# A three-stage kernel (attention, dense layer, top-2 mixture of experts): the list table in bfloat16 parts, the last batch's routing spread, the first expert's low halves on GpSimd

## The chip, the cores and the metric

The kernel runs on one core of a Trainium2 chip. The metric is device time in microseconds (us), the median over runs of one program. TensorE (PE in the profile, with its weight loads as PEld), VectorE (DVE), ScalarE (ACT), GpSimd (POOL) and SyncE (SP, which here only issues transfers) each work through a queue of their own, in order, and meet at semaphores.

## The reference, cut to what matters

```python
def _moe2_ref(x, w_gate, w_noise, noise, w1, w2):
    logits = x @ w_gate
    noisy_logits = logits + np.log1p(np.exp(x @ w_noise)) * noise
    top2 = np.argpartition(-noisy_logits, 2, axis=1)[:, :2]
    ...                                   # softmax over the two: top2_w
    for e in range(E):
        for k in range(2):
            mask = top2[:, k] == e
            ...
            h = np.maximum(x[mask] @ w1[e], 0.0)
            out[mask] += top2_w[mask, k, None] * (h @ w2[e])

def reference(q, k, v, phi, moe_w_in, moe_w_out, ...):
    x = _attn_ref(q, k, v, phi)           # 4 batches x 576 tokens, 8 heads x 64
    x = _moe_ref(x, moe_w_in, moe_w_out)  # 512 -> 2048 -> 512, leaky relu 0.01
    return _moe2_ref(x, ...)              # 8 experts, 512 -> 1024 -> 512
```

There are 2304 tokens of 512 values. `moe_w_in` and `moe_w_out` are 64-bit floats and are converted on the chip; the rest is float32.

## The kernel before, in words

**Precision.** A large product is done in three passes over two parts of each operand, a high part (ACT copies the value to the type fp32r) and a low part (what is left, one subtraction on DVE or GpSimd): high by high, high by low, low by high. For the weights of the experts this is lines 802 to 809: `w2h` on ACT (L807), `w2l` on DVE (L808). A "high" and a "low" below mean these two instructions. Each expert has eight slices of its hidden layer (f = 0 to 7), each slice two weight tiles, so 16 highs and 16 lows an expert. SP loads the weights for two slices at a time in two transfers (L790 for `w1`, L792 for `w2`) into two pairs of staging buffers (`r1`, `r2`), so the next pair's transfers wait until both parts of the pair before last have been made from a buffer.

**Stage one** is the attention and the dense layer. The dense layer runs over 128 slots, in sixteen groups (four chunks of the hidden layer, times four batches) of eight (two halves u of a batch, times four slices). A slot is `l1` (six 288-column matmuls L587, then L593, L598, L603, L608) and, two slots later, `l2` (twelve 288-column matmuls L625). In the last chunk, whenever a half batch has its last slot done, its routing (`post`, lines 643 to 766) is put up as a job.

**Routing.** One `post` covers 288 tokens: the gate product (`pg` L650, `pl` L656), a transposed copy of the tokens to a table `x2` in DRAM (`px` L665, ACT L666, transfers L667), then on DVE the noisy logits, the top two, the rank of each token in its expert's list by a running count `cnt` (L709, L711), the row and the block of the list place (L723 to L730), and the weights. The list table `acc` (128 rows by 40 blocks, five blocks an expert) is then built by a product of one-hot matrices: `at` (place in the block, L736) against `va` (block one-hot, L753, times token number and times weight, L758 and L760), six float32 products `pi` (L764) that PE runs as twelve matmuls, added to `acc` by L766. `places` (L768 to L772) turns the token numbers in `acc` into gather indices `get` and scatter indices `put`.

**Stage two** runs the experts. For expert 0 its lists are cut in two: the first 360 places can be filled by batches 0 to 2 alone, so its first eight steps need only these; the rest needs the last batch. `early` (lines 1063 to 1071) does `places(0, 3)`, three row gathers on GpSimd (`fetch`, L820) and three `turn`s (four transposes `pxt` L833, `xh` on ACT L835, `xl` on DVE L836). Then come the steps `e1` (twelve matmuls L858, ACT L861, DVE L862) and `e2` (L876). `handover` makes `places` for all other blocks and fetches the rows for the second part, whose `turn` stands at step 8 (L1201).

**What sets the order.** Jobs have a start time, a due time and a cost; `tick(t)` (L127) takes steps of every job that is behind its straight line from t0 to t1, the earliest due first, at a cost of two a tick at most. There are two ticks a slot (L1145 and L639) and three a step of stage two (L1208, where t runs from 130 at 1.4 a step). The jobs for the last batch's halves are put up with t0 = n + 2 and t1 = n + 4 for their last slot n (123 and 127). This gives the order of the program; the tile framework's scheduler then lays down each engine's queue from it, and may put a later instruction earlier where it takes an engine to be free. `pg`, `pl`, `px`, `pr`, `pi` and `pxt` all share two banks of PSUM (tag "m"). The expert weights are split ahead of need (`WAT`, L1092): slices f = 0 to 3 of expert 0 during the last 22 slots, f = 4 to 7 around the end of stage one, where they take over the buffers of the dense layer's last weights, and the first slices of expert 1 right behind.

```python
Job(post(b, u), 10, n + 2, n + 2 + TP, 1)              # L641, TP = 2
nc.vector.tensor_sub(l_, src, h_.bitcast(F32))         # L808
Job(early(), 7, n - 0.1, n + 5, 0)                     # L1154, n = 124
```

Of the kernel before, what the change touches and what calls it, by code (L numbers as in the profile page):

```python
# [7 lines left out]
F32 = mybir.dt.float32  # L8
F32R = mybir.dt.float32r
BF = mybir.dt.bfloat16  # L10
I32 = mybir.dt.int32
# [9 lines left out]
def moe_kernel(  # L21
# [17 lines left out]
    nc = tc.nc  # L39
# [26 lines left out]
    BIG = 1 << 20  # L66
    scale = 1.0 / float(D) ** 0.5
# [223 lines left out]

    chosen = consts.tile([P, 2 * B, 3, 2 * HJ], F32)

    def late_consts():
        nc.vector.tensor_scalar(ups, jp[:P, :P], 0.0, None, op0=OP.is_gt)
        nc.vector.memset(onesb, 1.0)
        nc.vector.tensor_add(sel, ident[:, 0:2 * E], ident[:, 32:32 + 2 * E])
        for i in (64, 96):
            nc.vector.tensor_add(sel, sel, ident[:, i:i + 2 * E])
        nc.vector.memset(wgn, 0.0)  # L300
        for i, src in enumerate((w_gate, w_noise)):
            nc.gpsimd.dma_start(wgn[:, :, i * E:(i + 1) * E], src.rearrange("(c p) e -> p c e", p=128))
        nc.gpsimd.dma_start(nz.rearrange("p b j e -> p b (j e)"), noise.rearrange("(b p j) e -> p b (j e)", b=B, j=J))
        nc.gpsimd.iota(io8, pattern=[[1, E]], base=0, channel_multiplier=0, allow_small_or_imprecise_dtypes=True)
        nc.gpsimd.iota(tok, pattern=[[S, B], [1, J]], base=1, channel_multiplier=J, allow_small_or_imprecise_dtypes=True)
        nc.vector.memset(cnt, 0.0)
# [327 lines left out]
    def l2(n):  # L634
        b, u, f = slots[n]
        for db in range(NDB):
            l2_db(n, db)
            if db == 1:
                tick(n + 2.5)  # L639
        if f == F1 // 128 - 1:  # L640
            Job(post(b, u), 10, n + 2, n + 2 + TP, 1)  # L641

    def post(b, u):
# [25 lines left out]
        ez, uu, dd, t2 = (sm([HJ, E], nm) for nm in ("ez", "uu", "dd", "t2"))  # L669
# [31 lines left out]
        for j in range(HJ):  # L701
# [3 lines left out]
                         skip_group_check=True)  # L705
        rk = sm([HJ, E], "rk")
# [11 lines left out]
        ro = sm([2, HJ, E], "ro")  # L718
# [12 lines left out]
        at = [pp.tile([P, DM], F32, name="xr", bufs=4) for _ in range(2)]  # L731
        n4 = DM // 128
        at = [at[i // n4][:P, i % n4 * 128:(i % n4 + 1) * 128] for i in range(2 * HJ)] + at
        for i, t in ((0, at[-2]), (n4, at[-1])):
            n_ = min(n4, 2 * HJ - i)
            nc.vector.tensor_tensor(t[:P, :n_ * 128].rearrange("p (i r) -> p i r", i=n_),  # L736
                                    io128[:, None, :].to_broadcast([P, n_, 128]),
                                    pos[:, i:i + n_, None].to_broadcast([P, n_, 128]), op=OP.is_equal)
# [10 lines left out]
        ta = sm([2 * HJ, NT], "ta")  # L749
        nc.vector.tensor_tensor(ta, io128[:, None, 0:NT].to_broadcast([P, 2 * HJ, NT]),  # L750
                                blk[:, :, None].to_broadcast([P, 2 * HJ, NT]), op=OP.is_equal)
        ea = at[-1][:P, DM - 2 * HJ * E * NT:].rearrange("p (i e t) -> p i e t", i=2 * HJ, e=E)
        nc.vector.tensor_tensor(ea, oh.rearrange("p k j e -> p (k j) e")[:, :, :, None].to_broadcast([P, 2 * HJ, E, NT]),  # L753
                                ta[:, :, None, :].to_broadcast([P, 2 * HJ, E, NT]), op=OP.mult)
        va = pp.tile([P, DM], F32, name="xr", bufs=4)[:, :4 * HJ * E * NT].rearrange("p (i f x) -> p i f x", i=2 * HJ, f=2)
        eb = ea.rearrange("p i e t -> p i (e t)")
# [38 lines left out]
    def weights(order, split):  # L795
        ahead = [ld_w(*order[0])]
        yield
        for i, (e, fp) in enumerate(order):
# [82 lines left out]
    def combine(e, c, t):  # L881
        col, sz = tiles(e, c)[t]
        wcol = acc[:sz, 1, col:col + 1]
# [217 lines left out]
    for n in range(8, len(slots) + 2):  # L1101
# [21 lines left out]
        if n == PP:  # L1123
# [150 lines left out]
```

## Time and profile before

| | us |
|---|---|
| median of 3 runs | 939.47 (938.67 to 939.86) |
| the profiled execution, its own time | 937.07 |
| its span, first to last instruction | 935.2 |
| PE busy | 880.1 (94%) |
| DVE busy | 539.1 (58%) |
| ACT busy | 356.4 (38%) |
| POOL busy | 212.6 (23%) |
| chain that ended last: PE share | 80% |
| chain that ended last: DVE share | 10% |
| mean granted TensorE clock | 0.986 |

The profile is of one execution. Busy times are of the engine's own instructions. The page cuts the span into 40 equal slices of 23.4 us and gives the busy share of each in tenths, and PEclk, the clock that TensorE was granted, in tenths of full speed (2.4 GHz; 5 is 1.2 GHz). The chain that ended last is followed back from the last instruction to what released each step. In a timeline each row has the start, the duration (for several merged instructions, first start to last end), engine, line, operation, names, shapes; in brackets stands how long the engine had been idle and what ended that.

### The profile page before, as it was taken

The numbers are of one execution on the slowest core, as the hardware profiler recorded it, in microseconds if no ns is written. First come the engines' busy times: TensorE is split into PE (matmuls) and PEld (weight loads), VectorE is DVE, ScalarE is ACT, GpSimd is POOL, SyncE is SP. The second block draws the span as 40 slices with busy tenths as digits, with TensorE's granted clock in tenths as the row PEclk, the third lists the DMA queues.
The fourth block names the chain that finished last, engine by engine and source line by source line (L and its number), as shares of the span: only waits on it lengthen the run. The fifth ranks groups of instructions, "written<-read, shape, count | busy, mean of one in ns | idle before, by whom it ended". The sixth has DMA issues, their size and how long they took to land.

```text
span 935.2 us, 16252 instructions
## 1 busy us (share of the span) xinstructions
PE 880.1 (94%) x6344; PEld 786.5 (84%) x6344; DVE 539.1 (58%) x1294; ACT 356.4 (38%) x784; POOL 212.6 (23%) x207
## 2 busy tenths in 40 slices
PE   3588999999999999999699999999999999999996
PEld 2377788998999998889588889988988898899885
DVE  5798985456466868788754633544435454452312
ACT  2355665444444544454423433332333323331110
POOL 0051135334300110001003240422305133150302
PEclk9999999999999999999699999999999999999999
DMA  9988712021521201213623652523525434240211
GB/s 221 262 195 179 175 47 90 21 70 46 194 100 46 81 13 49 71 55 90 200 64 110 192 179 91 198 102 129 171 90 181 132 105 167 90 134 1 72 29 57
DMA packets 82615, 105.31 MB, mean 113 GB/s; under 512 B 23988, under 2 KB 58836, under 8 KB 82528
## 3 DMA queue, kind: packets, MB, share of 16 engines
q1 hardware_dynamic: 70528, 71.58, 26.6%
q0 software_dynamic: 9312, 27.88, 9.0%
q10 hardware_dynamic: 2688, 4.72, 1.6%
q8 instruction: 52, 0.85, 0.4%
q14 instruction: 35, 0.29, 0.1%
HBM read 85.88 MB, written 19.53 MB: 113 GB/s over the span
## 4 chain that ended last, share of the span: by engine, by line
PE 80%; DVE 10%; DMA 3%; issue 2%; ACT 2%; SPq 2%; POOL 0%; POOLq 0%; DVEq 0%; ACTq 0%
PE py L876 23%; PE ph L858 23%; PE py L625 18%; PE ph L587 9%; PE pvw L552 2%; PE pxt L833 2%; DMA big<-in_moe_w_out_dram 1%; PE pi L764 1%; DVE mx L360 1%; PE pg L650 1%; DVE mx L330 1%; SPq L194 1%; SPq L173 1%; DMA row<-x,get 1%; DVE wi L214 1%
## 5 line engine op out<-in xcount | busy, mean ns | idle before, releaser
L625 PE MATMUL py<-gh,woh 128*128 128x288 f32 x512 | 155.7, 304 | 3.5 <-ACT gh L603 1.9
L858 PE MATMUL ph<-xh,w2h 128*128 128x256 f32 (+1 forms) x512 | 157.2, 307 | 1.0 <-ACT xh L835 0.6
L858 PE MATMUL ph<-xh,w2l 128*128 128x256 f32 (+1 forms) x512 | 156.7, 306 | 0.0
L858 PE MATMUL ph<-xl,w2h 128*128 128x256 f32 (+1 forms) x512 | 156.1, 305 | 0.0
L808 DVE TENSOR_TENSOR w2l<-r,w2h 128x512 fp32r<-128x512 f32 x128 | 87.6, 687 | 115.5 <-ACT w2h L807 56.6
L625 PE MATMUL py<-gl,woh 128*128 128x288 f32 x512 | 153.3, 299 | 0.4 <-POOL gl L608 0.4
L625 PE MATMUL py<-gh,wol 128*128 128x288 f32 x512 | 152.5, 298 | 0.0
L861 ACT ACTIVATE gh<-ph 128x256 fp32r<-128x256 f32 (+1 forms) x128 | 54.5, 426 | 196.3 <-PE ph L858 186.3
L876 PE MATMUL py<-w2h,gh 128*128 128x512 f32 (+1 forms) x320 | 129.3, 404 | 0.0
L807 ACT ACTIVATE w2h<-r 128x512 fp32r<-128x512 f32 x128 | 79.3, 628 | 128.5 <-PE py L876 96.1
L876 PE MATMUL py<-w2h,gl 128*128 128x512 f32 (+1 forms) x320 | 126.2, 394 | 0.0
L876 PE MATMUL py<-w2l,gh 128*128 128x512 f32 (+1 forms) x320 | 126.1, 394 | 0.0
L862 DVE SCALAR_TENSOR_TENSOR gl<-ph,gh 128x256 fp32r<-128x256 f32 (+1 forms) x128 | 60.6, 473 | 112.3 <-ACT gh L861 103.7
L625 PEld LDWEIGHTS py<-gh,woh 128*128 128x128 f32 x512 | 97.0, 190 | 21.8 <-issue 16.6
L820 POOL DMA_INDIRECT row<-x,get x40 | 44.9, 1122 | 266.7 <-DVE put L771 150.0
L858 PEld LDWEIGHTS ph<-xh,w2h 128*128 128x128 f32 x512 | 97.2, 190 | 7.0 <-ACT xh L835 1.2
L858 PEld LDWEIGHTS ph<-xl,w2h 128*128 128x128 f32 x512 | 97.1, 190 | 3.3 <-DVE xl L836 0.2
L625 PEld LDWEIGHTS py<-gl,woh 128*128 128x128 f32 x512 | 96.9, 189 | 2.5 <-issue 1.4
L625 PEld LDWEIGHTS py<-gh,wol 128*128 128x128 f32 x512 | 97.1, 190 | 1.3 <-issue 1.3
L858 PEld LDWEIGHTS ph<-xh,w2l 128*128 128x128 f32 x512 | 97.0, 189 | 0.0
L598 DVE TENSOR_TENSOR sm<-ph,sm 128x288 f32<-128x288 f32 x128 | 57.7, 451 | 62.4 <-ACT sm L593 61.9
L608 POOL TENSOR_TENSOR gl<-sm,gh 128x288 fp32r<-128x288 f32 x64 | 60.1, 942 | 114.2 <-ACT gh L603 98.2
(163 smaller groups left out, 1520.2 us busy)
## 6 DMA issues: line engine op xcount, KB each, us to landing
r<-in_moe_w_dram SPq DMA_DIRECT2D x64, 512.0 KB, 3.8
raw<-in_moe_w_in_dram SPq DMA_DIRECT2D x16, 512.0 KB, 4.0
raw<-in_moe_w_out_dram SPq DMA_DIRECT2D x14, 512.0 KB, 4.2
out_dram<-zr SPq DMA_DIRECT2D x18, 256.0 KB, 3.8
x<-xr ACTq DMA_DIRECT2D x24, 192.0 KB, 2.2
q<-in_q_dram SPq DMA_DIRECT2D x21, 192.0 KB, 5.0
phi<-in_phi_dram SPq DMA_DIRECT2D x8, 288.0 KB, 3.3
kv<-in_k_dram SPq DMA_DIRECT2D x6, 384.0 KB, 6.6
```

The lines of the kernel that those rows point to most:

```text
L552: nc.tensor.matmul(VW[b, c][g][hp * M:(hp + 1) * M, :], VT[b][g * 64:(g + 1) * 64, 1, hp * M:(hp + 1) * M], WI[c, hp][g * 64:(g + 1) * 64, ...
L587: nc.tensor.matmul(ph, w_[:, o:o + 128], a_[:, g], start=(t == 0), stop=(t == 5))
L598: nc.vector.tensor_tensor(sm, ph, sm, op=OP.max)
L608: (eng or (nc.gpsimd if n < NPOOL else nc.vector)).tensor_sub(lo, sm, hi.bitcast(F32))
L625: nc.tensor.matmul(py, w_[:, s], g_, start=(first and i == 0), stop=(last and i == 2))
L807: nc.scalar.activation(h_, src, AF.Copy)
L808: nc.vector.tensor_sub(l_, src, h_.bitcast(F32))
L820: nc.gpsimd.indirect_dma_start(out=xg[:sz], out_offset=None, in_=x2[:(B - 1) * S] if (e, c) == (0, 0) else x2, in_offset=bass.IndirectOffs ...
L858: nc.tensor.matmul(ph[:, :n], w_[:, s], x_[:, db], start=(t == 0), stop=(t == 3 * NDB - 1))
L861: nc.scalar.activation(hi, ph[:, :n], AF.Relu)
L862: nc.vector.scalar_tensor_tensor(lo, ph[:, :n], 0.0, hi.bitcast(F32), op0=OP.max, op1=OP.subtract)
L876: nc.tensor.matmul(PY[c, t][:sz], h_[:, o:o + sz], w_, start=(f == 0 and i == 0), stop=(f == NF2 - 1 and i == 2))
```

## The change

The change has three parts.

1. The list table in bfloat16 parts. `acc` has five fields of 40 blocks where it had two: the token number as two parts (its value shifted right by 8, and its low 8 bits), and the weight as three bfloat16 parts. The one-hot matrix `at` is written as bfloat16 by one instruction over 768 elements, where two wrote float32 over 512 and 256. `val` collects the five values of each choice (six small instructions). `va` is made by two products over 600 elements, all bfloat16. `pi` is six bfloat16 matmuls of 200 columns. `places` first puts the parts together again (three more instructions, L768 ff.), and the combining step reads the weight from field 2. Constants for the token parts are made once, in `late_consts`. `ez`, `uu`, `dd`, `t2` and `ro` have one buffer instead of two.
2. The last batch's routing. `post` has one more yield (11 steps), and the two jobs of the last batch get t0, t1 = 127, 132 and 131.5, 136 where they had 125, 127 and 129, 131.
3. The lows of expert 0 go to GpSimd.

```diff
+            t0, t1 = {(B - 1, 0): (n + 4, n + 9), (B - 1, 1): (n + 4.5, n + 9)}.get((b, u), (n + 2, n + 2 + TP))
+            Job(post(b, u), 11, t0, t1, 1)
-            Job(post(b, u), 10, n + 2, n + 2 + TP, 1)
...
-        at = [pp.tile([P, DM], F32, name="xr", bufs=4) for _ in range(2)]
...
-            nc.vector.tensor_tensor(t[:P, :n_ * 128].rearrange("p (i r) -> p i r", i=n_),
-                                    io128[:, None, :].to_broadcast([P, n_, 128]),
-                                    pos[:, i:i + n_, None].to_broadcast([P, n_, 128]), op=OP.is_equal)
+        at = pp.tile([P, DM], F32, name="xr", bufs=4).bitcast(BF)[:, :2 * HJ * 128].rearrange("p (i r) -> p i r", r=128)
+        nc.vector.tensor_tensor(at, io128[:, None, :].to_broadcast([P, 2 * HJ, 128]),
+                                pos[:, :, None].to_broadcast([P, 2 * HJ, 128]), op=OP.is_equal)
...
+        val = sm([2, HJ, NV], "val", BF)
+        for i in range(2):
+            nc.vector.tensor_copy(val[:, i, :, 0:2], tokp[:, :, b, u * HJ:(u + 1) * HJ].rearrange("p f j -> p j f"))
+        wr = sm([2, HJ], "wr")
+        nc.vector.tensor_copy(val[:, :, :, 2], kj(1))
+        nc.vector.tensor_sub(wr, kj(1), val[:, :, :, 2])
+        nc.vector.tensor_copy(val[:, :, :, 3], wr)
+        nc.vector.tensor_sub(val[:, :, :, 4], wr, val[:, :, :, 3])
...
+        yield 0
+        va = [t[:, :HJ * NV * E * NT].rearrange("p (j f x) -> p j f x", j=HJ, f=NV) for t in vt]
         for i in range(2):
-            nc.vector.tensor_mul(va[:, i * HJ:(i + 1) * HJ, 0], eb[:, i * HJ:(i + 1) * HJ],
-                                 tok[:, b, u * HJ:(u + 1) * HJ, None].to_broadcast([P, HJ, E * NT]))
-        nc.vector.tensor_mul(va[:, :, 1], eb, ch[:, 1, :, None].to_broadcast([P, 2 * HJ, E * NT]))
+            nc.vector.tensor_tensor(va[i], ea[:, i * HJ:(i + 1) * HJ].rearrange("p j e t -> p j (e t)")[:, :, None, :]
+                                    .to_broadcast([P, HJ, NV, E * NT]),
+                                    val[:, i, :, :, None].to_broadcast([P, HJ, NV, E * NT]), op=OP.mult)
         yield 1
         pi = ps_m("pi")
         for i in range(2 * HJ):
-            nc.tensor.matmul(pi[:, :2 * E * NT], at[i], va[:, i].rearrange("p f x -> p (f x)"), start=(i == 0),
+            nc.tensor.matmul(pi[:, :NV * E * NT], at[:, i], va[i // HJ][:, i % HJ].rearrange("p f x -> p (f x)"), start=(i == 0),
                              stop=(i == 2 * HJ - 1))
-        nc.vector.tensor_add(acc, acc, pi[:, :2 * E * NT].rearrange("p (f x) -> p f x", f=2))
+        nc.vector.tensor_add(acc, acc, pi[:, :NV * E * NT].rearrange("p (f x) -> p f x", f=NV))

     def places(c0, c1):
         ac, no = acc[:, 0, c0:c1], put[:, c0:c1].bitcast(F32)
+        nc.vector.scalar_tensor_tensor(ac, ac, 256.0, acc[:, 1, c0:c1], op0=OP.mult, op1=OP.add)
+        for f in (3, 2):
+            nc.vector.tensor_add(acc[:, f, c0:c1], acc[:, f, c0:c1], acc[:, f + 1, c0:c1])
...
-                    nc.vector.tensor_sub(l_, src, h_.bitcast(F32))
+                    (nc.gpsimd if e == 0 else nc.vector).tensor_sub(l_, src, h_.bitcast(F32))
...
-        wcol = acc[:sz, 1, col:col + 1]
+        wcol = acc[:sz, 2, col:col + 1]
...
-            acc = pp.tile([128, 2, E * NT], F32, name="acc")
+            acc = pp.tile([128, NV, E * NT], F32, name="acc")
-            io128 = pp.tile([P, 128], F32, name="io128")
+            io128 = pp.tile([P, 128], BF, name="io128")
```

## Rows read from the trace of the kernel before

**Rows 1.** The page: PE's busy share and the granted clock in 40 slices

```profile
PE   3588999999999999999699999999999999999996
PEclk9999999999999999999699999999999999999999
```

**Rows 2.** Windows: engines' busy us (instructions), granted clock, DMA share, GB/s

```profile
340.00:440.00 100.00, 98.42 (x788) 86.94 (x787) 80.14 (x375) 44.65 (x111) 0.10 (x1) 1.00 0.19 58
...
448.00:449.00 1.00, 0.71 (x6) 0.48 (x4) 1.00 (x7) 1.00 (x3) 0.00 (x0) 1.00 0.00 0
...
451.00:452.00 1.00, 0.00 (x0) 0.00 (x0) 1.00 (x4) 0.00 (x0) 0.00 (x0) 0.53 0.75 139
...
468.00:469.00 1.00, 1.00 (x11) 0.92 (x12) 0.43 (x2) 0.65 (x2) 0.00 (x0) 0.94 0.54 207
```

**Rows 3.** Timeline of PE from stage one's last matmuls to stage two's first

```profile
448.29 0.29 PE L625 MATMUL py<-gl,woh 128*128 128x288 f32 x1
448.42 0.29 PE L625 MATMUL py<-gh,wol 128*128 128x288 f32 x1
455.62 2.82 PE L764 MATMUL pi<-xr 96*128 96x80 f32 x12 [6.91 <-DVE xr L760]
458.23 1.92 PE L833 MATMUL pxt<-ident,row 128*128 128x128 f32 x8
...
462.27 0.67 PE L858 MATMUL ph<-xh,w2h 128*128 128x360 f32 x1 [0.61 <-ACT xh L835]
```

**Rows 4.** Timeline of DVE: first and last of expert 0's eight late lows

```profile
442.88 0.68 DVE L808 TENSOR_TENSOR w2l<-r,w2h 128x512 fp32r<-128x512 f32 x1
...
454.09 0.68 DVE L808 TENSOR_TENSOR w2l<-r,w2h 128x512 fp32r<-128x512 f32 x1
```

**Rows 5.** Timeline of ACT over the same stretch

```profile
445.65 3.74 ACT L807 ACTIVATE w2h<-r 128x512 fp32r<-128x512 f32 x7
453.80 0.63 ACT L807 ACTIVATE w2h<-r 128x512 fp32r<-128x512 f32 x1 [4.41 <-DMA r<-in_moe_w_dram]
455.11 1.67 ACT L807 ACTIVATE w2h<-r 128x512 fp32r<-128x512 f32 x3 [0.69 <-DMA r<-in_moe_w_dram]
457.40 0.63 ACT L807 ACTIVATE w2h<-r 128x512 fp32r<-128x512 f32 x1 [0.61 <-DMA r<-in_moe_w_dram]
459.33 0.60 ACT L835 ACTIVATE xh<-pxt 128x512 fp32r<-128x512 f32 x1 [1.30 <-PE pxt L833]
```

**Rows 6.** Timeline of SP: the weight transfers issued after stage one

```profile
450.07 0.37 SPq L790 DMA_DIRECT2D r<-in_moe_w_dram  x1
450.74 0.37 SPq L792 DMA_DIRECT2D r<-in_moe_w_dram  x1
453.91 0.37 SPq L790 DMA_DIRECT2D r<-in_moe_w_dram  x1
```

**Rows 7.** POOL: its last gather before stage two; subtractions of L238, ns min/median/max

```profile
442.53 1.90 POOL L820 DMA_INDIRECT row<-x,get  x1 [0.30 <-issue]
...
L238 POOL TENSOR_TENSOR wol<-wi,woh x16: 1286/1300/2100, 47.4 to 328.3; 128x512 fp32r<-128x512 f32 x16
```

**Rows 8.** The chain (pi, pxt), and PE's timeline around four bfloat16 matmuls

```profile
482.27 1.36 PE pi L764 x12
...
499.91 0.87 PE pxt L833 x8
...
446.15 0.30 PE L702 MATMUL pr<-hit,onesb 96*96 96x24 bf16 x3
...
446.35 0.38 PE L625 MATMUL py<-gh,wol 128*128 128x288 f32 x1
```

**Rows 9.** Groups on DVE by shape: count, busy us, mean ns

```profile
L736 DVE TENSOR_TENSOR xr<-io,pos 96x512 f32<-96x512 f32 x8 | 5.4, 680 | 0.0
...
L758 DVE TENSOR_TENSOR xr<-xr,tok 96x120 f32<-96x120 f32 x16 | 3.8, 274 | 0.1
...
L760 DVE TENSOR_TENSOR xr<-xr,chosen 96x240 f32<-96x240 f32 x8 | 3.2, 398 | 0.0
...
L728 DVE CAST pos<-ri 96x6 f32<-96x6 int32 x8 | 1.3, 166 | 0.1
```

More of the change, by code (lines that the diff above doesn't have):

```diff
@@ L66, in moe_kernel @@
     BIG = 1 << 20
+    NV = 5
     scale = 1.0 / float(D) ** 0.5
@@ L290, in moe_kernel @@
     cnt = consts.tile([P, E], F32)
+    tokp = consts.tile([P, 2, B, J], BF)
     chosen = consts.tile([P, 2 * B, 3, 2 * HJ], F32)
@@ L305, in late_consts @@
         nc.gpsimd.iota(tok, pattern=[[S, B], [1, J]], base=1, channel_multiplier=J, allow_small_or_imprecise_dtypes=True)
+        ti = wt("ti", F32).bitcast(I32)[:P, :2 * B * J].rearrange("p (f b j) -> p f b j", f=2, b=B)
+        nc.vector.tensor_copy(ti[:, 0], tok)
+        nc.vector.tensor_scalar(ti[:, 1], ti[:, 0], 255, None, op0=OP.bitwise_and)
+        nc.vector.tensor_scalar(ti[:, 0], ti[:, 0], 8, None, op0=OP.logical_shift_right)
+        nc.vector.tensor_copy(tokp, ti)
         nc.vector.memset(cnt, 0.0)
@@ L640, in l2 @@
         if f == F1 // 128 - 1:
-            Job(post(b, u), 10, n + 2, n + 2 + TP, 1)
+            t0, t1 = {(B - 1, 0): (n + 4, n + 9), (B - 1, 1): (n + 4.5, n + 9)}.get((b, u), (n + 2, n + 2 + TP))
+            Job(post(b, u), 11, t0, t1, 1)
+    ranked = []
     def post(b, u):
@@ L667, in rows @@
             nc.scalar.dma_start(x2[b * S:(b + 1) * S].rearrange("(p j) d -> p j d", j=J)[:, u * HJ + j, :], xr)
-        ez, uu, dd, t2 = (sm([HJ, E], nm) for nm in ("ez", "uu", "dd", "t2"))
+        ez, uu, dd, t2 = (sm([HJ, E], nm, bufs=1) for nm in ("ez", "uu", "dd", "t2"))
         nc.scalar.activation(ez, lg[:, :, E:2 * E], AF.Exp)
@@ L705, in post @@
                          skip_group_check=True)
+        ranked.append((b, u))
+        assert ranked == sorted(ranked)
         rk = sm([HJ, E], "rk")
@@ L716, in kj @@
             return ch[:, f].rearrange("p (k j) -> p k j", k=2)
-        ro = sm([2, HJ, E], "ro")
+        ro = sm([2, HJ, E], "ro", bufs=1)
         nc.vector.tensor_mul(ro, oh, rk[:, None, :, :].to_broadcast([P, 2, HJ, E]))
@@ L748, in post @@
         nc.vector.tensor_copy(kj(2), ef)
-        ta = sm([2 * HJ, NT], "ta")
+        val = sm([2, HJ, NV], "val", BF)
[6 more added lines that the diff above has]
+        nc.vector.tensor_sub(val[:, :, :, 4], wr, val[:, :, :, 3])
+        ta = sm([2 * HJ, NT], "ta", BF)
         nc.vector.tensor_tensor(ta, io128[:, None, 0:NT].to_broadcast([P, 2 * HJ, NT]),
                                 blk[:, :, None].to_broadcast([P, 2 * HJ, NT]), op=OP.is_equal)
-        ea = at[-1][:P, DM - 2 * HJ * E * NT:].rearrange("p (i e t) -> p i e t", i=2 * HJ, e=E)
+        vt = [pp.tile([P, DM], F32, name="xr", bufs=4).bitcast(BF) for _ in range(2)]
+        ea = vt[1][:, 2 * DM - 2 * HJ * E * NT:].rearrange("p (i e t) -> p i e t", i=2 * HJ, e=E)
         nc.vector.tensor_tensor(ea, oh.rearrange("p k j e -> p (k j) e")[:, :, :, None].to_broadcast([P, 2 * HJ, E, NT]),
                                 ta[:, :, None, :].to_broadcast([P, 2 * HJ, E, NT]), op=OP.mult)
-        va = pp.tile([P, DM], F32, name="xr", bufs=4)[:, :4 * HJ * E * NT].rearrange("p (i f x) -> p i f x", i=2 * HJ, f=2)
-        eb = ea.rearrange("p i e t -> p i (e t)")
+        yield 0
+        va = [t[:, :HJ * NV * E * NT].rearrange("p (j f x) -> p j f x", j=HJ, f=NV) for t in vt]
         for i in range(2):
-            nc.vector.tensor_mul(va[:, i * HJ:(i + 1) * HJ, 0], eb[:, i * HJ:(i + 1) * HJ],
-                                 tok[:, b, u * HJ:(u + 1) * HJ, None].to_broadcast([P, HJ, E * NT]))
-        nc.vector.tensor_mul(va[:, :, 1], eb, ch[:, 1, :, None].to_broadcast([P, 2 * HJ, E * NT]))
+            nc.vector.tensor_tensor(va[i], ea[:, i * HJ:(i + 1) * HJ].rearrange("p j e t -> p j (e t)")[:, :, None, :]
+                                    .to_broadcast([P, HJ, NV, E * NT]),
+                                    val[:, i, :, :, None].to_broadcast([P, HJ, NV, E * NT]), op=OP.mult)
         yield 1
```

4 lines of the change are left out of this document (removed).

## The prediction

> **What bounds the kernel now.** I read the page first, then the stretch that stands out in it, engine by engine. The page says that PE is nearly always busy, but for the two ends, and at the full clock, but for one slice, the twentieth (444 to 468 us), where both PE and the clock drop to 6 tenths [rows 1]. Elsewhere only less work for PE can help: in the 100 us before that slice PE was busy 98.4% and DVE 80% [rows 2]. The slice is the handover from stage one to stage two. PE's last stage-one matmul starts at 448.42; then PE stands for 6.91 us, does `pi` and the transposes of the first gathered rows, and begins stage two only at 462.27 [rows 3]. The granted clock falls to its lower level, 1.2 GHz, about 451.1, some 2.4 us after PE's last matmul, and comes back about 468.1 [rows 2]. `pi` took 2.82 us there, 1.36 at the full clock [rows 3, 8].
>
> What PE waited for is DVE: the last batch's first half of routing and, mixed into it, eight lows of expert 0, from 442.88 to 454.09 [rows 4]. But a second queue ends nearly as late. The gathers were issued by 444.4 [rows 7] and no transfer was moving in 448 to 449 [rows 2], so the gathered rows had long landed. The first `xh` still came only at 459.33, because ACT's queue holds, ahead of it, seven highs of expert 0 and five of expert 1, and those five wait for weights: at 453.80, 455.11 and 457.40 the wait that ends is that of a transfer [rows 5]. These transfers were issued at 450.07, 450.74 and 453.91 [rows 6], each when lows had freed a staging buffer. `xh` itself was released by PE, but had PE been ready it could not have started before about 458.0, when the fifth of those highs ends. So the handover has two limits, DVE through `pi`, and lows, transfers, highs through ACT, and the change takes hold of the first.
>
> **Part one, the list table.** PE: twelve matmuls of 1.36 us become six of 200 columns. Stage one's 288 columns come every 0.13 us [rows 3], so 200 take 0.09 and six 0.55. Four bfloat16 matmuls of few columns, weight loads included, let the next instruction start 0.20 us after them [rows 8], 0.05 each, so weight loads are no floor above that. The ends are nothing gained (loads that do not hide) and 0.81 a half batch; I take 0.8, nearest to these rows. Eight half batches are routed. Six lie in the stretch where PE is 98.4% busy, one in stage two, where it is again the chain [rows 8]; the eighth stood in the gap and is counted below. Seven times 0.8 is **5.6 us**.
>
> DVE, for each half batch: `at` as one instruction costs about what two did. An instruction's slope is 680 less 398 ns over 272 elements [rows 9], about 1.04 ns an element, so each `va` of 600 elements takes some 0.77 us, 1.5 for both, against 0.27 twice and 0.40 before. `val` is six small instructions of 0.16 [rows 9], 0.6 to 1.0. Add 0.1 for a wider L766: DVE gets about 1.4 us more a half batch, 8.4 for six. Four of expert 0's slices leave DVE over the same stretch, eight lows of 0.68, so DVE goes from 80 to about 83 of 100. I cost this at nothing; what hides it is that PE runs at 98%, and if the cover is gone it costs at most the 8.4 us.
>
> `places` gets three instructions, some 0.6 us, and the batch before last's second half 0.6 more net of its shorter `pi`: the three gathers come about 1.2 us later and the rows land by about 449 to 450, far ahead of `xh`. The fields to `places` and the one-buffer tiles (half batches follow each other more than 10 us apart) cost nothing.
>
> **Part two, the later due times.** The first half's `pg`, `pl`, `px` (twelve transposes, three copies and three transfers to `x2` on ACT's queue), `pr` and `pi` now fall behind the turns. PE does the same work later: what leaves stage one's tail comes back in stage two, so this is nil but for the place of `pi`: it leaves the gap, and PE need not wait for that routing before the transposes. It costs 0.55 in stage two. The second half's `pi`, at 482.27, moves one to two steps later; its rows are first needed at 499.91 [rows 8], so some 10 us still cover the gathers and their landing.
>
> **Part three, the lows on GpSimd.** GpSimd is free: 0.10 us busy in the 100 us before [rows 2]. A subtraction of the same shape takes 1.30 there, against 0.68 on DVE [rows 7, 4]. The Trainium skill, GPSIMD Engine Reference, section Engine selection, says to keep two-input elementwise work on VectorE, being about twice as slow on GpSimd; the trace agrees, 1.9 times. What matters is who waits for these lows: not the matmuls of expert 0 (its slice 4 is five steps off), but SP's transfers for expert 1, and behind these ACT's highs, and behind these `xh`.
>
> So I follow that queue. The first late low stands behind the third gather, at about 445.6 (444.4 and 1.2). At 1.30 each the third is done at 449.5, the fourth at 450.8, the fifth at 452.1. The `w1` transfer is free after the third (449.5; before 450.07), the `w2` transfer after the fourth or fifth (450.8 to 452.1; before 450.74). The latter released ACT 4.4 us after its issue [rows 5, 6]: 455.2 to 456.5. Two highs of 0.56 need it: `xh` at 456.3 to 457.6. From `xh` to the first stage-two matmul it was 2.94 us [rows 5, 3]: 459.3 to 460.5. I take 459.7, which is **2.6 us** earlier than 462.27, with four of expert 1's highs ahead of `xh`, since the fifth waits for a later buffer. PE has then stood as long as before, so the clock drops and I leave its price as it is: 5.8 us at half rate, 2.9 lost.
>
> **The sum.** 5.6 + 2.6 - 0.55 = 7.6 us (rounded). The terms come from one execution of 937.07; the median is 2.4 above it, and I take the difference over: 939.47 - 7.6 = **931.9 us**. The smaller gain than the gap of 13 us is due to the second limit.
>
> **The rivals.**
>
> *xh goes first* (chance 0.22). With PE no longer waiting for `pi`, the scheduler may put the turns ahead of expert 1's highs. Then `xh` starts when the seven highs of expert 0 are done, 449.4 [rows 5], and the rows are there, say 449.8, and stage two at about 452.4: 9.9 us earlier, 2.9 more if the clock holds. 5.6 + 9.9 - 0.55 is 15.0, with the clock 17.9: 921.6 to 924.5. For it: the turns are now earlier in the program than that routing. Against: in the queue before, five of these highs stood ahead, and nothing in the change brings the rows sooner.
>
> *The fifth high stays ahead too* (0.18). It needs a buffer that the seventh low frees, 445.6 + 9.1 = 454.7; its transfer took 3.5 us [rows 6, 5], so it ends at 458.8 and stage two starts at 461.7: 5.6 + 0.6 - 0.55 = 5.6 us, 933.8. For it: that was the order before. Against: on GpSimd this buffer is freed later, which favours `xh`.
>
> *GpSimd's lows hold up ACT* (0.07), the slower side. One subtraction of L238 took 2.10 [rows 7]. If all eight do, with DVE working beside them, and all eight highs of expert 1 stand ahead of `xh`, the last buffer is free at 462.4, its weights are there at 466.8, `xh` starts at 467.9 and stage two at 470.8: 8.5 later, so 8.5 + 0.55 - 5.6 = 3.5 slower, 942.9. It decides from a mean of about 1.9 a low. Against: 15 of 16 such rows lie nearer 1.30. The Trainium skill, GPSIMD Engine Reference, section Specifications, has GpSimd share its SBUF interfaces with VectorE, contending with instructions of two SBUF inputs. By that rule this rival's price is right; the median row does not bear it out.
>
> *DVE becomes the limit of the routing stretch* (0.06). Then the 8.4 us come on PE's path: 7.6 less 8.4, about 940, no change. Against: DVE at 83%.
>
> **How the numbers follow.** The forecast has 0.47. A measurement here tells 0.2% (1.9 us) from no change, so faster means under 937.6. The forecast, *xh first* and nearly all of *the fifth high* are faster: 0.87. Same 0.07 (*DVE becomes the limit*, a rest of the others), slower 0.06. The forecast's own range is 929 to 934 (0.4 to 0.8 for `pi`, 459.3 to 460.5). The range reaches from *xh first* with a small rest below, 921, to 937, where `pi` gains half and nothing else does.
>
> **What would show it.** Right: `pi` in about 0.55 to 0.7 us; the lows of the 440s and 450s on GpSimd at 1.3; the transposes right behind stage one's last matmul; `xh` behind four highs that wait for weights; stage two's first matmul some 11 us after stage one's last; the clock still down. Wrong: that distance at 3 to 5 us (*xh first*) or above 14 (GpSimd's lows), PE idle between 340 and 440 for `va`, or a wait for the second part's rows at step 8.

## The result and the profile after

The change made the kernel slower: 949.7 us (median of 4 runs, 948.84 to 951.29) against 939.07 before on the same chip, a ratio of 1.0115 with a 95% interval of 1.0097 to 1.0132. The prediction was 931.9 in a range of 921 to 937, so both sign and range were wrong. The profiled execution took 949.78 us, its span is 947.9: 12.7 more than the span before.

The page first: PE's busy share and the granted clock in 40 slices, the kernel after.

```profile
PE   3588999999999999998599999999999999999996
PEclk9989999999999999998799999999999999999999
```

The dip of [rows 1] is still there and wider: PE is down in two slices, the nineteenth and twentieth (427 to 474 us), and so is the clock. PE's timeline shows the handover (stage one's matmuls are L632 here, stage two's L878):

```profile
461.54 0.29 PE L632 MATMUL py<-gh,wol 128*128 128x288 f32 x1
467.41 1.09 PE L853 MATMUL pxt<-ident,row 128*128 128x128 f32 x4 [5.58 <-DMA row<-x,get]
...
475.32 0.97 PE L878 MATMUL ph<-xh,w2h 128*128 128x360 f32 x2
```

From stage one's last matmul to stage two's first it is 13.78 us; before it was 13.85 [rows 3]. So the handover costs what it cost, though for another wait: no longer `pi`, but the gathered rows. What is lost lies in front of it: stage one ends 13.1 us later (461.54 against 448.42). After the handover nothing differs: from `ph` to the end it is 472.6 us, before 472.9.

Windows of stage one's second half (columns as in [rows 2]):

```profile
340.00:440.00 100.00, 94.17 (x680) 77.32 (x678) 76.60 (x328) 41.23 (x101) 10.13 (x8) 0.97 0.16 52
...
428.00:437.00 9.00, 7.24 (x38) 7.00 (x37) 7.73 (x31) 2.97 (x8) 2.56 (x2) 0.62 0.34 119
...
450.00:456.00 6.00, 2.73 (x21) 2.49 (x19) 6.00 (x10) 2.94 (x6) 5.79 (x4) 1.00 0.03 4
```

In 340 to 440 PE got through 680 matmuls where it did 788 [rows 2]; part one's shorter `pi` explains at most 36 of the 108 that are missing. It is idle for 5.8 of 100 us, and for part of 428 to 437 the clock stood at its lower level, 1.2 GHz (mean 0.62), after PE had waited 1.5 us for `hit`, up to 427.3, and while it waited 1.8 us for `sm`, up to 430.8; DVE makes both. In 450 to 456 PE was busy 2.73 of 6 us while DVE was busy throughout and GpSimd did four lows. DVE's timeline of that stretch, and GpSimd's:

```profile
450.30 1.23 DVE L740 CAST pos<-ri 96x6 f32<-96x6 int32 x1
451.44 0.15 DVE L762 TENSOR_TENSOR wr<-chosen,val 96x6 f32<-96x6 f32 x1
451.52 0.14 DVE L720 TENSOR_SCALAR cnt<-cnt 96x1 f32<-96x1 f32 x1
451.58 1.20 DVE L741 TENSOR_TENSOR blk<-blk,pos 96x6 f32<-96x6 f32 x1
452.71 0.94 DVE L744 TENSOR_TENSOR xr<-io,pos 96x768 bf16<-96x768 bf16 x1
453.58 1.22 DVE L742 TENSOR_SCALAR blk<-blk 96x6 f32<-96x6 f32 x1
454.72 0.16 DVE L763 CAST val<-wr 96x6 bf16<-96x6 f32 x1
454.79 1.52 DVE L615 TENSOR_TENSOR gl<-sm,gh 128x288 fp32r<-128x288 f32 x1
```

```profile
450.21 5.79 POOL L828 TENSOR_TENSOR w2l<-r,w2h 128x512 fp32r<-128x512 f32 x4 [17.07 <-DVE val L761]
```

Six elements take 1.2 us instead of 0.16: such an instruction lasts until the low that runs on GpSimd is over. For L615 PE waits 3.6 us, and behind that wait the clock stands at its lower level again (0.50 in 457 to 459). The groups show how much this adds to DVE's instructions, and what part one costs DVE:

```profile
L828 POOL TENSOR_TENSOR w2l<-r,w2h 128x512 fp32r<-128x512 f32 x16 | 21.0, 1328 | 111.9 <-ACT w2h L827 91.0 <-DVE val L761 17.1 <-PE py L632 3.8
...
L775 DVE TENSOR_TENSOR xr<-xr,val 96x600 bf16<-96x600 bf16 x16 | 11.8, 774 | 0.1
L744 DVE TENSOR_TENSOR xr<-io,pos 96x768 bf16<-96x768 bf16 x8 | 7.6, 947 | 0.0
L781 PE MATMUL pi<-xr 96*128 96x200 bf16 x48 | 7.2, 261 | 0.0
L686 DVE TENSOR_SCALAR dd<-uu 96x24 f32<-96x24 f32 x8 | 3.5, 432 | 0.2
...
L740 DVE CAST pos<-ri 96x6 f32<-96x6 int32 x8 | 2.4, 296 | 0.0
```

L740's counterpart before, L728, took 166 ns [rows 9], L686's 174. L775 is as dear as forecast, L744 a little cheaper (947 ns, where two instructions took 680 and 414). The lows themselves take 1282 ns at the median (1328 in the mean), no more than L238's 1300 [rows 7].

### The profile page after: what moved, and what is told of

The parts are those of the page before. It is cut to its first block, busy times and chain, and to the rows that moved or that the text cites. A ratio compares the mean times of both kernels' runs of the same rounds, so it can differ in the third digit from the quotient of the medians.

```text
span 947.9 us, 16212 instructions
## 1 busy us (share of the span) xinstructions
PE 884.1 (93%) x6296; PEld 782.2 (83%) x6296; DVE 551.5 (58%) x1320; ACT 355.9 (38%) x784; POOL 231.8 (24%) x223
## 4 chain that ended last, share of the span: by engine, by line
PE 81%; DVE 10%; DMA 3%; ACT 2%; SPq 2%; issue 1%; POOL 0%; POOLq 0%; ACTq 0%; DVEq 0%
PE py L896 24%; PE ph L878 23%; PE py L632 18%; PE ph L594 9%; PE pvw L559 2%; PE pxt L853 2%; DMA phi<-in_phi_dram 1%; PE pg L660 1%; DMA big<-in_moe_w_out_dram 1%; DVE mx L367 1%; DVE mx L337 1%; DVE sm L605 1%; SPq L174 1%; SPq L195 1%; DVE wi L215 1%
## 5 line engine op out<-in xcount | busy, mean ns | idle before, releaser
L632 PE MATMUL py<-gh,woh 128*128 128x288 f32 x512 | 156.1, 307 | 3.1 <-ACT gh L610 1.9
L632 PE MATMUL py<-gl,woh 128*128 128x288 f32 x512 | 154.3, 302 | 4.0 <-DVE gl L615 3.6
L878 PE MATMUL ph<-xh,w2h 128*128 128x256 f32 (+1 forms) x512 | 156.0, 305 | 0.2 <-issue 0.2
L878 PE MATMUL ph<-xh,w2l 128*128 128x256 f32 (+1 forms) x512 | 155.6, 304 | 0.0
L878 PE MATMUL ph<-xl,w2h 128*128 128x256 f32 (+1 forms) x512 | 155.3, 303 | 0.0
L632 PE MATMUL py<-gh,wol 128*128 128x288 f32 x512 | 154.3, 302 | 0.0
L828 DVE TENSOR_TENSOR w2l<-r,w2h 128x512 fp32r<-128x512 f32 x112 | 76.8, 687 | 116.1 <-ACT w2h L827 54.6
L632 PEld LDWEIGHTS py<-gh,woh 128*128 128x128 f32 x512 | 98.0, 192 | 19.8 <-issue 13.5
L632 PEld LDWEIGHTS py<-gl,woh 128*128 128x128 f32 x512 | 97.9, 191 | 6.0 <-DVE gl L615 3.9
L632 PEld LDWEIGHTS py<-gh,wol 128*128 128x128 f32 x512 | 98.3, 192 | 4.0 <-issue 4.0
L878 PEld LDWEIGHTS ph<-xh,w2h 128*128 128x128 f32 x512 | 96.6, 189 | 5.1 <-issue 0.5
L878 PEld LDWEIGHTS ph<-xl,w2h 128*128 128x128 f32 x512 | 96.5, 189 | 3.3 <-DVE xl L856 0.2
L878 PEld LDWEIGHTS ph<-xh,w2l 128*128 128x128 f32 x512 | 96.5, 188 | 0.0
L615 POOL TENSOR_TENSOR gl<-sm,gh 128x288 fp32r<-128x288 f32 x64 | 60.1, 941 | 115.3 <-ACT gh L610 107.4
L610 ACT ACTIVATE gh<-sm 128x288 fp32r<-128x288 f32 x128 | 56.5, 443 | 76.6 <-DVE sm L605 76.6
```

The costliest lines, as they stand in the source:

```text
L610: nc.scalar.activation(hi, sm, AF.Copy)
L615: (eng or (nc.gpsimd if n < NPOOL else nc.vector)).tensor_sub(lo, sm, hi.bitcast(F32))
L632: nc.tensor.matmul(py, w_[:, s], g_, start=(first and i == 0), stop=(last and i == 2))
L828: (nc.gpsimd if e == 0 else nc.vector).tensor_sub(l_, src, h_.bitcast(F32))
L878: nc.tensor.matmul(ph[:, :n], w_[:, s], x_[:, db], start=(t == 0), stop=(t == 3 * NDB - 1))
```

## The experiments

Every run below was compared with the kernel before on its own chip. The table has, of each profiled execution, the time of the sixth of the eight sums into `acc` (L766 before, L783 after; with it `places` can start), of the first transpose of gathered rows, and of stage two's first matmul.

| kernel | median us | ratio, 95% interval | sixth sum | first `pxt` | first `ph` |
|---|---|---|---|---|---|
| before | 937.7 to 939.1 | 1 | 438.9 | 458.2 | 462.3 |
| after | 949.70 | 1.0097 to 1.0132 | 460.5 | 467.4 | 475.3 |
| parts 1, 2 | 943.50 | 1.0039 to 1.0082 | 449.8 | 458.1 | 465.9 |
| part 1 | 946.89 | 1.0071 to 1.0110 | 451.4 | 469.3 | 474.3 |
| part 3 | 946.53 | 1.0071 to 1.0105 | 443.2 | 468.3 | 472.8 |
| part 2 | 926.56 | 0.9855 to 0.9888 | 440.1 | 444.5 | 450.9 |
| parts 2, 3 | 934.32 | 0.9951 to 0.9984 | 444.8 | 449.2 | 459.2 |
| part 2, filler | 947.77 | 1.0096 to 1.0130 | 456.1 | 462.0 | 469.3 |
| parts 1, 2, no extra step | 942.05 | 1.0027 to 1.0061 | 452.7 | 460.9 | 467.8 |
| parts 1, 2, light table | 940.29 | 1.0018 to 1.0051 | 453.0 | 460.7 | 467.3 |
| parts 1, 2, precedence | 931.50 | 0.9912 to 0.9957 | 443.7 | 449.9 | 457.3 |
| parts 2, 3, quarters | 933.62 | 0.9946 to 0.9978 | 442.8 | 447.2 | 458.4 |
| parts 1, 3 | 955.41 | 1.0159 to 1.0198 | 461.5 | 480.1 | 485.1 |
| light table, precedence | 938.17 | 0.9989 to 1.0010 | 445.8 | 451.9 | 461.0 |

From `ph` to the end of the span it is 470 to 475 us in every row: what differs is when stage two starts. Where stage one ends tells the two prices apart. Its last matmul starts at 448.4 before, at 447.3 with part one and 445.7 with parts one and two, but at 457.4 with part three and 459.1 with parts two and three. So part one lengthens the handover (20.2 us with parts one and two, 13.85 before), and part three lengthens stage one.

**The parts, two and one at a time.** The first drops part three from the kernel after:

```diff
-                    (nc.gpsimd if e == 0 else nc.vector).tensor_sub(l_, src, h_.bitcast(F32))
+                    nc.vector.tensor_sub(l_, src, h_.bitcast(F32))
```

> The changed kernel with the lows of expert 0 back on VectorE (parts one and two alone). Theory A (the port): while a GpSimd low runs, some VectorE instructions cannot finish and last 1.2 us instead of 0.16; then without these lows no VectorE row of L731 to L742 or L787 is above 0.4 us, the 3.6 us wait of L632 for L615 and the late gathers go, and the time falls by 8 to 12 us to 938 to 942, near the kernel before or under it. Theory B (the queue order): the routing's place in PE's and DVE's queues, set by the yield and the due times, is what costs; then the time stays at 946 to 951. Theory C (VectorE's load): the 1.5 us more of VectorE work a half batch is on PE's path; then PE's idle time in 340 to 440 stays at 5 us or more and the time is 944 to 948.

The second drops part two as well, which leaves part one:

```diff
-            t0, t1 = {(B - 1, 0): (n + 4, n + 9), (B - 1, 1): (n + 4.5, n + 9)}.get((b, u), (n + 2, n + 2 + TP))
+            t0, t1 = n + 2, n + 2 + TP
             Job(post(b, u), 11, t0, t1, 1)
```

> The bfloat16 table alone: lows of expert 0 on VectorE, due times as before. Theory A: 5.6 us of PE time saved, little of it lost, 933 to 937. Theory C: VectorE's 1.5 us more a half batch eats the saving, 938 to 944. Theory B, which blames the due times, expects 933 to 937 as A does.

The third is the kernel before with the lows of expert 0 on GpSimd, part three alone:

```diff
-                    nc.vector.tensor_sub(l_, src, h_.bitcast(F32))
+                    (nc.gpsimd if e == 0 else nc.vector).tensor_sub(l_, src, h_.bitcast(F32))
```

> The kernel before with only the lows of expert 0 on GpSimd. Theory A: VectorE rows that read two-port forms or two tiles of SBUF stretch to 1.2 us while a low runs, and the time rises by 2 to 10 us, 941 to 949. Theories B and C: VectorE loses 16 x 0.68 us of work and the handover's gap shrinks, 933 to 938.

The fourth is the kernel before with the later due times, part two alone:

```diff
-            Job(post(b, u), 10, n + 2, n + 2 + TP, 1)
+            t0, t1 = {(B - 1, 0): (n + 4, n + 9), (B - 1, 1): (n + 4.5, n + 9)}.get((b, u), (n + 2, n + 2 + TP))
+            Job(post(b, u), 10, t0, t1, 1)
```

> The kernel before with only the two later due times. Theory B: the order gets worse, 942 to 948. Theories A and C: the handover no longer waits for pi but is held by expert 1's highs on ACT, 935 to 938.

Each of parts one and three alone makes the kernel some 8 us slower; part two alone makes it 12 faster and beats both kernels. So theory A is right about part three and wrong about part one, for which it and theory B had 933 to 937; theory C has part one's sign, but its 938 to 944 is too low, and the idle time that it names for parts one and two did not come (2.2 us in 340 to 440, where it had 5 or more); part two's 926.6 lies outside every range. Part two's PE timeline has no handover gap left:

```profile
448.50 0.29 PE L625 MATMUL py<-gh,wol 128*128 128x288 f32 x1
449.77 0.55 PE L834 MATMUL pxt<-ident,row 104*128 104x104 f32 x4 [0.98 <-DVE big L628]
...
450.44 0.29 PE L625 MATMUL py<-gh,wol 128*128 128x288 f32 x1
450.92 0.43 PE L859 MATMUL ph<-xh,w2h 128*128 128x360 f32 x1 [0.19 <-ACT xh L836]
```

Stage two follows 0.5 us behind stage one's last matmul, and the clock stays at its higher level (1.00 in 446 to 470, where before it was 0.50 in 452 to 468). ACT's timeline tells why:

```profile
445.18 0.60 ACT L836 ACTIVATE xh<-pxt 128x512 fp32r<-128x512 f32 x1 [0.99 <-PE pxt L834]
...
446.14 1.14 ACT L808 ACTIVATE w2h<-r 128x512 fp32r<-128x512 f32 x2
447.37 0.60 ACT L836 ACTIVATE xh<-pxt 128x512 fp32r<-128x512 f32 x1
...
450.35 0.52 ACT L836 ACTIVATE xh<-pxt 128x416 fp32r<-128x416 f32 x1 [1.76 <-PE pxt L834]
...
455.43 0.62 ACT L808 ACTIVATE w2h<-r 128x512 fp32r<-128x512 f32 x1
```

The turns run among stage one's last matmuls, 4 us after `places`. Some highs stand between the `xh`, but none that waits for weights, and after the last `xh` the next high comes 5 us later.

Part three alone shows the hold at its plainest. DVE, then GpSimd:

```profile
454.81 1.31 DVE L726 CAST ri<-blk 96x6 int32<-96x6 f32 x1
...
456.16 1.22 DVE L727 TENSOR_SCALAR ri<-ri 96x6 int32<-96x6 int32 x1
...
457.42 1.19 DVE L728 CAST pos<-ri 96x6 f32<-96x6 int32 x1
458.64 1.18 DVE L729 TENSOR_TENSOR blk<-blk,pos 96x6 f32<-96x6 f32 x1
```

```profile
454.80 9.44 POOL L808 TENSOR_TENSOR w2l<-r,w2h 128x512 fp32r<-128x512 f32 x7 [3.68 <-ACT w2h L807]
```

Seven lows hold up seven instructions of the last batch's routing, one each (four are shown); PE then waits 8.0 us for that routing's `pi`, where the kernel before waits 6.9. The greater part of the price was paid by then: stage one ends 9.0 us later, and in it PE waits 5.8 us for `hit`, 1.5 before. PE never waits for a low. So part three's price is what GpSimd does to VectorE, not where the lows stand in a queue; part one's was still open, between VectorE's load, the extra step and the queues' order.

**Parts two and three.** Part two alone, with the lows on GpSimd:

```diff
-                    nc.vector.tensor_sub(l_, src, h_.bitcast(F32))
+                    (nc.gpsimd if e == 0 else nc.vector).tensor_sub(l_, src, h_.bitcast(F32))
```

> Parts two and three, the table in float32. Theory P (a low on GpSimd holds VectorE: one VectorE instruction of 0.16 us waits for the whole of a 1.27 us low, so VectorE's routing work stretches): part three costs here what it cost alone, 944.4 - 935.2 = 9 us of span, on top of part two's 923.6, so about 930 to 934 of time, with VectorE instructions of the small kind at 1.1 to 1.3 us wherever lows run and TensorE waiting for VectorE, not for a low. Rival G (what hurts is that the handover's gathers stand behind lows in GpSimd's queue, or that the lows come late): TensorE waits for a low or for a gather before the first matmul of stage two, and the VectorE instructions keep 0.16 us. Rival N (part two takes the routing's last half batches off the path, so nothing is left for the lows to hold up): within 1.5 us of 926.6.

934.32: 7.8 above part two alone (8.9 by the ratios, since the two ran on different chips), so the two add up, as theory P has it, and with no handover gap the price is paid in stage one. PE waits for `hit` 4.3 us before `ph`, 1.5 in part two alone, and 1.9 for L598, where part two alone does not wait: 4.7 of the 8.3 us by which `ph` comes later. One DVE instruction was held longer than any low lasts; DVE, then GpSimd:

```profile
451.11 3.63 DVE L608 TENSOR_TENSOR gl<-sm,gh 128x288 fp32r<-128x288 f32 x1
```

```profile
449.41 5.00 POOL L809 TENSOR_TENSOR w2l<-r,w2h 128x512 fp32r<-128x512 f32 x4
```

It came during the second of the four lows. Its operands were there by 450.80 (ACT's `gh`), and it ends 0.33 us after the last low, which ends at 454.41. Lows back to back, 1.25 us each, did not let it in between, though beside the seven lows of part three alone each instruction was let in after one; what makes the difference is not shown.

**A filler on VectorE.** Part two alone, with four products behind `ea`:

```diff
+        for _ in range(4):
+            nc.vector.tensor_tensor(ea, ea, ea, op=OP.mult)
```

> Part two, the table in float32, and four more VectorE products of ea with itself (96x240, 0.40 us each, starting 0.32 apart, values unchanged) between the making of ea and the table's columns: about 1.3 us more in each half batch's VectorE chain, nothing more on TensorE. Theory S (the half batches of the routing follow one another without slack, each waits for the one before, so a delay in each adds up over the six that stage one holds, and the places and gathers come late): the acc sum of the sixth half batch, 440.1 in part two alone, comes at about 446 to 449, the first transpose of the gathered rows later by as much, and the time is 930 to 936. Rival V (VectorE has room and slack is there; part one is dear for another reason, its extra step or its order in the queues): the sixth sum within 2 us of 440, the time within 1.5 us of 926.6.

The sixth sum came 16 us later, not 6 to 9, and the time rose by 21: rival V is out, and theory S has the direction but about half the size. More work for VectorE alone, without bfloat16, extra step or change on PE, does what part one does. Each of the four products keeps VectorE's queue for 0.32 us, 7.7 us for six half batches, so each microsecond of work makes the sixth sum two later. With part one it is the same: the table further below finds 4.7 us of its own work, and against part two alone the sum comes 9.7 us later.

**Without the extra step.** Parts one and two, with the step and its count taken out:

```diff
-        yield 0
         va = [t[:, :HJ * NV * E * NT].rearrange("p (j f x) -> p j f x", j=HJ, f=NV) for t in vt]
```

> Parts one and two without the extra step that part one adds to each half batch's routing (the sums of the table are issued with ea, and the job counts 10 steps as before). Theory S (the VectorE chain's length): no better than parts one and two, 941 to 945, the sixth acc sum still at 447 to 450. Rival V (the extra step makes the routing late): the sixth sum returns to 441 to 443 and the time to 922 to 928.

No difference beyond the spread (942.05 against 943.50): the extra step is not the cause.

**A lighter table.** The same, with four columns and the token's parts held ready:

```diff
-    NV = 5
+    NV = 4
...
-        val = sm([2, HJ, NV], "val", BF)
+        val = vals[:, 2 * b + u]
```

> Parts one and two without the extra step, with the table's columns made lighter: the token's two parts stand ready from the start, and the weight has two bfloat16 parts in place of three, so four columns of 40 in place of five (96x480 in place of 96x600) and four VectorE instructions fewer in each half batch; the third part of the weight is left out. By theory S the chain loses about 0.3 us in the sums and 0.3 to 0.5 in small ones: the sixth acc sum comes 3 to 5 us earlier than with five columns (449.8 there), and the time is 932 to 940, between parts one and two and part two alone. Rival V: no different from the run without the extra step, within 1.5 us.

A miss for theory S: with less VectorE work the sixth sum is no earlier (453.0, without the extra step 452.7), and the time, 940.29, lies just above its range. The time between ranks (L721) and sum, added over the six half batches of stage one, tells where the length comes from; the routing's own instructions, others (stage one's, and lows) that stand between them in VectorE's queue, and idle time:

| kernel | ranks to sum, six | routing's own | others between | idle |
|---|---|---|---|---|
| before | 43.6 us | 23.9 | 16.0 (41 instructions) | 3.7 |
| parts 1, 2 | 53.5 | 28.6 | 23.6 (60) | 1.3 |
| light table | 51.3 | 25.5 | 24.1 (60) | 1.7 |
| parts 1, 2, precedence | 46.9 | 27.6 | 19.4 (51) | 0.0 |

Part one's own work is 4.7 of the 9.9 us. The larger share is other instructions that now stand in between, 7.6 us, less 2.4 of idle time, and with the light table they are as many. About half of the nineteen more come with the length alone: at the rate of the kernel before, 41 in 43.6 us, 53.5 us would hold 50. The rest is the queue's order. On PE too the place moved: before, the sixth half batch's `pi` stands behind 2259 of stage one's 2304 matmuls, with part one behind all 2304.

**The order alone.** Parts one and two, the stretch from the ranks on given precedence:

```diff
+        with tc.high_priority(offset=400):
+            rk = sm([HJ, E], "rk")
...
```

> Parts one and two with the same instructions, but the routing's part from the ranks to the table's sum is given precedence where the queues are ordered, so that fewer of stage one's VectorE instructions stand between the ranks and the sum: 7, 7, 10, 8, 9, 10 in the six half batches where parts one and two have 7, 8, 9, 10, 13, 13 and part two alone 7, 5, 7, 5, 10, 7; on TensorE the sixth half batch's list matmuls stand behind 2282 of stage one's 2304 matmuls, where they stood behind all 2304, and behind 2259 in part two alone. Theory O (the place in the queues decides, VectorE's own added 0.8 us per half batch is the smaller part): the sixth acc sum at 443 to 447, where parts one and two have 449.8, the wait for the gathered rows shorter than 8.4 us by that much, the time 930 to 939. Theory S (the added VectorE work itself decides): the sixth sum at 448 to 451 and the time within 2 us of 943.

Theory O holds, in the time and in the sixth sum (443.7): with the same instructions the time falls from 943.5 to 931.5. PE's waits from 430 to 480 in parts one and two, then with precedence:

```profile
PE pxt L853 <- DMA row<-x,get: 8.4, 1, 8.4
PE pi L781 <- DVE xr L775: 2.9, 2, 2.6
```

```profile
PE pxt L858 <- DMA row<-x,get: 2.8, 1, 2.8
```

Not all of the 8.4 us is the table's lateness. Late gathers also landed slower: a median of 6.8 us after their issue with parts one and two, beside weight transfers issued from 449.85 on, 4.2 with precedence and 3.5 in part two alone. That the weight transfers slow them is not shown.

Still, it is 5 us behind part two alone, whose `pi` is longer: the rows come 2.8 us late, and the clock falls to its lower level again (0.55 and 0.50 in 450 to 455 and 455 to 460).

**Lows in quarters.** Parts two and three, each low cut in four:

```diff
+                        for c in range(NDB):
...
+                            nc.gpsimd.tensor_sub(lo[:, c_], s_, hi[:, c_].bitcast(F32))
```

> Parts two and three with each low on GpSimd cut into four instructions of 128x128 on the same data; the queues' order is that of parts two and three. Theory P (a VectorE instruction waits out the GpSimd instruction that runs, so the wait is as long as that one): the long VectorE instructions fall from 1.1 to 1.3 us to 0.3 to 0.5 us, and the time comes a good part of the way from 934.3 to part two's 926.6, to 927 to 932. Rival L (the lows on GpSimd cost because they are late or because GpSimd and VectorE share a bandwidth that both use up): the same work is done over the same time, so 933 to 937.

A miss for theory P in the time (933.62, by its interval no different from 934.32, and inside rival L's range), a hit in the small instructions. Groups on DVE, 346 to 460, with whole lows and with quarters:

```profile
L608 DVE TENSOR_TENSOR gl<-sm,gh 128x288 fp32r<-128x288 f32 x27 | 16.3, 604 | 0.5 <-ACT gh L603 0.5
...
L672 DVE TENSOR_SCALAR uu<-ez 96x24 f32<-96x24 f32 x7 | 3.4, 484 | 0.0
```

```profile
L608 DVE TENSOR_TENSOR gl<-sm,gh 128x288 fp32r<-128x288 f32 x27 | 16.9, 625 | 0.5 <-ACT gh L603 0.5
...
L672 DVE TENSOR_SCALAR uu<-ez 96x24 f32<-96x24 f32 x7 | 2.0, 283 | 0.0
```

L672, 172 ns in part two alone, falls from 484 to 283, since it now waits out 0.43 us. L608 doesn't: it was held once through eleven quarters in a row. DVE, then GpSimd:

```profile
449.17 4.77 DVE L608 TENSOR_TENSOR gl<-sm,gh 128x288 fp32r<-128x288 f32 x1
```

```profile
447.36 6.89 POOL L813 TENSOR_TENSOR w2l<-r,w2h 128x128 fp32r<-128x128 f32 x16
```

It came during the fifth quarter and ends at 453.94, 0.32 us after the fifteenth; the sixteenth, 0.66 us in place of 0.44, waits for it. Four quarters take 1.72 us where one low took 1.25, so the run lasts longer. PE waits 3.1 us for `hit`, 4.3 with whole lows, but 2.2 for `lg`, which stands behind L608 in VectorE's queue, 1.0 with whole lows: what it gains at the small ones it loses here. So the time fell in rival L's range for another reason than the rival's: PE waits for no low, and a bandwidth that both engines share would not make an instruction of 0.45 us last 4.77. Whether pauses in GpSimd's run would help wasn't tried.

**Parts one and three.** The kernel after, without the later due times:

```diff
-            t0, t1 = {(B - 1, 0): (n + 4, n + 9), (B - 1, 1): (n + 4.5, n + 9)}.get((b, u), (n + 2, n + 2 + TP))
+            t0, t1 = n + 2, n + 2 + TP
             Job(post(b, u), 11, t0, t1, 1)
```

> Parts one and three with the due times of before. If the parts' costs add as they did alone (part one 946.9, part three 946.5, before 938.4): 955. If part two's gain of 12 us were still there in the whole change, this kernel would stand 12 above it, 962. If the two delays overlap, since both make the same sixth half batch late and the handover waits for it once: 948 to 953, and part two's later due times are worth less than 4 us in the whole change.

955.41: the two prices add. By the ratios (1.0178 and 1.0115) part two is then worth 6 us in the whole change, where it is 12 alone, 11 with part three (1.0088 and 0.9967), and 3.4 with part one. Where the table is late, there are no rows to turn at stage one's end: with parts one and two the sixth sum comes 4.1 us after stage one's last matmul, in part two alone 10.4 before it.

**Light table with precedence.** The light table, the whole routing given precedence:

```diff
+        with tc.high_priority(offset=400):
+            y = Y[:, 2 * b + u]  #S
...
```

> The lighter table of four columns (the weight's third part left out), without the extra step, part two's due times, lows on VectorE, and precedence for the whole of the routing: the sixth half batch's list matmuls stand behind 2277 of stage one's 2304. Theory O: the sixth acc sum at 442 to 446, and TensorE, which does 5 us less, reaches the handover with a gap of 3 to 8 us: 924 to 933, perhaps the level of part two alone. Theory S: no better than the light table without precedence, 938 to 942.

The sixth sum comes at 445.8, as theory O has it, but the time misses, 938.17, and lies in theory S's range: PE waits 3.6 us for rows and 1.6 for L681's copies of the last batch. That precedence for the whole routing puts these copies ahead of the turns is argued, not shown. Part two alone stays the best.

## Why the prediction was wrong

**Part one, PE.** The mechanism was right, the size a little off: six matmuls go in two groups of 0.36 us, 0.72 in place of 1.36, so 0.64 a half batch where 0.8 was taken, 4.5 us in place of 5.6.

**Part one, DVE: the step that failed most.** "I cost this at nothing; what hides it is that PE runs at 98%". The size of the instruction was right (0.77 us for a `va` instruction, 0.774 measured), the 1.4 us a half batch too high: in the queue, where one starts before the last has ended, the routing's own work grew by 0.8. What the step left out is that this work lies on a chain. PE's share did cover the load in stage one: with parts one and two PE was busy 97.8% in 340 to 440 (98.4 before), and stage one ended 2.8 us earlier. But the half batches of the routing follow one another. The next one's gate product starts 0.1 us before to 3.3 after the sum of the last in the kernel before, 1.1 before to 3.2 after with parts one and two, so what is added between ranks and sum is paid once for each. The six grew by 9.9 us, and "the three gathers come about 1.2 us later" became 10.8 (438.9 to 449.8 for the sum ahead of them). The routing fell behind stage one, and the handover waited for the rows. The rival *DVE becomes the limit*, at 0.06, had the right engine, but not the place, and its bound of 8.4 was too low: with part one added part two alone goes from 926.56 to 943.50.

**Part two.** "The handover has two limits" did not last: the second, highs of expert 1 ahead of `xh`, held only in the queue of before. With the turns early in the program, the `xh` come ahead of the highs that wait for weights, as the rival *xh goes first* said: stage two at 450.9 in part two alone, the rival had 452.4. In the kernel after too, ACT stands idle for 5.96 us before its first `xh`, for `pxt` and not for weights. Without part one, and with `pi` in stage two at its old 1.36 us, that rival's sum is a gain of 8.5 to 11.4 us; part two alone gained 11.9.

**Part three.** "What matters is who waits for these lows" looked at the wrong side. PE and `xh` wait for no low; VectorE's instructions wait for GpSimd. The row of 2.10 us among L238's sixteen was read as the lows becoming slower, and the mean of about 1.9 us at which that rival decides did not come (1.33). The trace of before had the other side as well. Beside L238's subtractions on GpSimd one VectorE instruction of 0.43 us (L209's median) lasted 1.43, to 0.3 us past the end of the second subtraction:

```profile
143.40 2.89 POOL L238 TENSOR_TENSOR wol<-wi,woh 128x512 fp32r<-128x512 f32 x2
145.15 1.43 DVE L209 TENSOR_SCALAR wi<-wi 128x512 int32<-128x512 int32 x1 [0.90 <-ACT wi L203]
```

The Trainium skill, SBUF — State Buffer, section Who interferes with whom, says that the two engines lock a pair of ports for a whole instruction and that whoever comes second stands still. The traces agree for 1.2 us beside a low of 1.27; the prediction used the rule in one direction only.

**The sum.** By the parts alone (8.5, 8.1 and -11.9 us) one would have 4.7 us slower. The whole change is 10.6 slower, since with part one in place half of part two's gain is gone. The forecast's 7.6 us faster had part one's 5.6 and the handover's 2.6, and nothing for either price.

Left open is why the order of the queues shifts as it does with a longer table; that it does is shown by the table of the ranks, and that the order alone is worth 12 us by the run with precedence.

## What to carry to other kernels

Before work is added off the critical engine, look whether it lies on a chain that repeats, and multiply its price by the links; VectorE's busy share of 80% said nothing of that here. Before work goes to GpSimd, ask what VectorE does beside it, not who waits for the result. And a change of three parts is tried part by part: here the one that touched two lines held all of the gain.

## What was not expected of the hardware

- A VectorE instruction with both operands in SBUF can be held by several GpSimd instructions in a row: 3.63 us beside three lows and 4.77 us beside eleven quarters, for 0.45 us of work. Cutting the lows up did not let it in sooner. Others were let in after one low (1.15 to 1.31 us); why these were not is open.
- Instructions that read PSUM were not held: in the same stretch L628 took 445 ns with lows on GpSimd and 442 without, L598 447 and 449, and the L628 at 459.93 in parts two and three, wholly inside a low, took 0.43 us. By the section of the Trainium skill named above, an instruction with one SBUF input outside the faster modes does not contend; the rows agree.
- It goes both ways: in the kernel after, the third of the four lows ran from 452.73 to about 454.8, 2.05 us, while L744 (0.94 us, from 452.71) went first.
